# One transformer block in float32 on one core: three layer-norm transposes moved from TensorE to VectorE and HBM, and tiles 5 to 8 reordered

## The chip, the core and the metric

The kernel runs on one core of a Trainium2 chip. The core has five engines, each with its own instruction queue that is worked off in program order: TensorE (PE) multiplies matrices and writes to PSUM, VectorE (DVE) and ScalarE (ACT) do elementwise work, GpSimd (POOL) does some more of it, and SyncE (SP) issues the transfers between HBM and on-chip memory. Engines wait for one another through semaphores. The metric is the device time of one launch in microseconds (us); smaller is better. The kernel before takes 554.39 us, the median of 3 runs (554.28 to 555.3).

## The reference, cut to what matters

The input x has 2048 tokens of 512 channels. A modulation vector of six parts is made from c; then a linear attention with 32 heads of 16 channels is added to x, and then a bilinear feed-forward network of width 1376. Both have a modulated layer norm in front.

```python
mod = (_silu(c) @ w_mod).reshape(c.shape[0], 6, 1, -1)
sa, ca, ga, sb, cb, gb = (mod[:, 0], mod[:, 1], ..., mod[:, 5])
h = _layernorm(x) * (1 + ca) + sa                    # first layer norm
q, k, v = split(h @ wqkv)                            # 32 heads of 16
phi = lambda t: jnp.where(t > 0, t + 1, jnp.exp(t)) + 1e-6
kv = einsum("bhsd,bhse->bhde", phi(k), v);  z = sum over s of phi(k)
o = (phi(q) @ kv) / (phi(q) . z + 1e-6)
x = x + ga * (o @ wo)
h = _layernorm(x) * (1 + cb) + sb                    # second layer norm
x = x + gb * (((h @ w_gate) * (h @ w_up)) @ w_down)
```

## The kernel before, in words

The 2048 tokens lie in four chunks (0 to 3) of four tiles of 128 tokens, so there are tiles 0 to 15. Every float32 product is computed from a high part h, rounded to the format that TensorE reads fast, and a low part l, the rest: h by h, h by l and l by h, so three matmuls for each 128 channels of depth. A product of one tile with a 512 by 512 weight has twelve matmuls (`product`, L203).

A product needs the normalized activations with channels on the partitions, and they come with tokens on the partitions. So each chunk's norm is transposed. In `Norm.transpose` (L289) TensorE turns sixteen blocks of 128 by 128 for a chunk, four for each of the four channel groups k, into a PSUM bank each; `Norm.modulated` (L302) scales and shifts the bank on ScalarE into f, casts f to h (VectorE or ScalarE) and takes l = f - h on VectorE.

The kernel has another way to turn a tile, used already for the queries of tiles 4 to 15 and for the second norm of chunks 2 and 3: the columns are written in an order that groups blocks of 32 (`xhat_blocks`, L275), the tile is stored to HBM, loaded back with its blocks of 32 rows moved to other partitions (`move_out`, `move_in`, L719 and L725: one store, four loads), and VectorE transposes the blocks of 32 by 32 (`turn_v` L733, `flip` L899). `flipped` (L904) then scales and shifts one channel group out of the four turned tiles in the buffer `wide`; it reads all four of them.

*The first loop (L525)* runs over the tiles i. TensorE does the key projection of tile i+2 (`proj(i + 2, wk)`), in passes 3, 4, 6 and 7 a query projection as well (`q_at`, L521), and then `t_tile(i)`, the twelve matmuls that add tile i's phi(k) times normalized x to the attention state. ScalarE and VectorE split the normalized x (`k_split_x`), split phi(k) (`k_split`), make phi of the projections (`k_phi`, `q_a`, `q_b`), add up phi (`z_add`) and do the jobs of `extra` (L509): splits of the value and output weights, and parts of the modulation vector (`mod_part`). The norm of chunk ch+1 is prepared inside chunk ch's passes: statistics in passes j = 2 and 3 of the chunk before, scale and offset for all four tiles at once (`rstd_of`, with a power on GpSimd, and `nmr_of`) in j = 3, the normalized tiles (`xhat`) in j = 3 and 0, and the transposes in j = 0 and 1, eight at a time, between the halves of `t_tile`. The key projection of tile 8 is the first that needs chunk 2, that of tile 12 the first that needs chunk 3.

*After the loop* the order of the work is written out by hand (L1207 on). `gate_up(ch, f)` makes the products with the gate and up weights for one of three lone column groups f0, f1, f2 of width 128, 128 and 96, and the function that it returns multiplies and splits them; `down` multiplies with the down weights. `y_step(i)` adds the attention output of tile i to x (`y_a`, twelve matmuls), readies the next tile and takes the row sums of the tile before for the second norm (`y_b`). `den_a`, `den_b` and `den_c` make the attention's denominators of a chunk and divide by them; `ready` is `den_c` and the store of `move_out`. `ln2_nx` and `ln2_turn` normalize and turn a chunk's second norm. From L1348 on a Strassen-like scheme works on the rest of the feed-forward columns (L1030), with operands kept in HBM (`kept`).

All work tiles share one pool of 94 buffers (`NB`), in PSUM there are 4 + 4 banks, and all transfers go through the queue of SyncE in program order.

## Time and profile before

| what | value |
|---|---|
| median of 3 runs | 554.39 us (554.28 to 555.3) |
| the profiled execution | 554.37 us |
| its span, first to last instruction | 552.7 us |
| TensorE busy | 547.0 us (99%) |
| VectorE busy | 373.6 us (68%) |
| ScalarE busy | 291.7 us (53%) |
| GpSimd busy | 203.4 us (37%) |
| HBM read, written | 42.60 MB, 15.20 MB |
| granted TensorE clock | full in every slice |

Busy times are of one profiled execution. A timeline row has the start in us from the first instruction, the duration, the engine, the line of the kernel, the operation and its tiles, and in brackets the idle time before it and what ended it. Matmuls are pipelined: a matmul of 512 columns is shown as 0.39 us, while the next one starts 0.23 us after it; the distance of starts is what counts. In the same way an operation of VectorE or ScalarE overlaps the end of the one before by about 0.1 us. L12 is line 12 of the kernel.

### The profile page before, as it was taken

How to read it: one execution, taken by the hardware profiler on the slowest of the kernel's cores; microseconds unless marked ns; L12 is line 12 of the kernel's file. 1: busy time of each engine (PE TensorE's matmuls, PEld its weight loads, DVE VectorE, ACT ScalarE, POOL GpSimd, SP SyncE). 2: the span in 40 equal slices, each digit the busy share in tenths (PEclk: the TensorE clock that was granted, in tenths of full speed). 3: DMA queues.
4: the chain of work that ended last, by engine and by line, in shares of the span. 5: the costliest groups of instructions: out<-in, count | busy, mean ns of one | idle time of the engine just before them, and what ended most of it. 6: DMA issues, size and time to landing. Idle time of an engine off the chain costs nothing.

```text
span 552.7 us, 7324 instructions
## 1 busy us (share of the span) xinstructions
PE 547.0 (99%) x2488; PEld 449.2 (81%) x2488; DVE 373.6 (68%) x610; ACT 291.7 (53%) x539; POOL 203.4 (37%) x204
## 2 busy tenths in 40 slices
PE   8999999999999999999999999999999999999997
PEld 7788888888888878878888888877888888888886
DVE  7896968986887886778776576985444444434434
ACT  3695856646476667566684545454443444444110
POOL 2000000102003201057596666766666546446200
PEclk9999999999999999999999999999999999999999
DMA  8900203320503205845545071690434222200004
GB/s 284 387 15 2 76 20 103 108 77 1 157 2 133 96 5 186 267 145 135 160 111 155 0 230 38 216 322 2 133 116 132 59 57 59 58 20 0 1 0 152
DMA packets 58373, 58.28 MB, mean 105 GB/s; under 512 B 7328, under 2 KB 38304, under 8 KB 58336
## 3 DMA queue, kind: packets, MB, share of 16 engines
q1 hardware_dynamic: 58336, 57.83, 33.2%
q8 instruction: 19, 0.31, 0.2%
q14 instruction: 18, 0.15, 0.1%
HBM read 42.60 MB, written 15.20 MB: 105 GB/s over the span
## 4 chain that ended last, share of the span: by engine, by line
PE 99%; DVE 0%; issue 0%
PE bank L1030 33%; PE acc L766 7%; PE acc L1110 6%; PE acc L1111 6%; PE acc L1112 6%; PE bank L207 5%; PE bank L209 5%; PE bank L208 5%; PE acc L375 3%; PE acc L374 3%; PE acc L373 3%; PE bank L849 2%; PE bank L851 2%; PE bank L850 2%; PE acc L146 2%; PE bank L293 2%
## 5 line engine op out<-in xcount | busy, mean ns | idle before, releaser
L1030 PE MATMUL bank<-h,w 128*128 128x512 f32 (+1 forms) x798 | 184.7, 390 | 0.0
L1030 PEld LDWEIGHTS bank<-h,w 128*128 128x128 f32 (+1 forms) x798 | 148.4, 186 | 33.4 <-ACT bank L1035 0.7
L1035 ACT ACTIVATE bank<-bank 128x512 f32<-128x512 f32 (+1 forms) x38 | 22.2, 583 | 139.6 <-PE bank L1030 139.5
L836 DVE TENSOR_TENSOR x<-acc,x 128x512 f32<-128x512 f32 (+1 forms) x73 | 48.8, 682 | 48.4 <-PE acc L1112 47.7
L1016 POOL TENSOR_TENSOR w<-raw,w 128x256 fp32r<-128x256 f32 (+3 forms) x38 | 40.9, 1077 | 91.0 <-ACT w L1009 91.0
L1111 PE MATMUL acc<-w,kh 128*128 128x512 f32 (+2 forms) x154 | 59.6, 387 | 0.0
L1110 PE MATMUL acc<-w,kh 128*128 128x512 f32 (+2 forms) x154 | 59.6, 387 | 0.0
L1112 PE MATMUL acc<-w,kl 128*128 128x512 f32 (+2 forms) x154 | 59.5, 386 | 0.0
L263 POOL TENSOR_TENSOR rstd<-ve,half 128x4 f32<-128x4 f32 (+1 forms) x10 | 11.0, 1103 | 121.8 <-DVE ve L262 69.6
L195 POOL TENSOR_TENSOR w<-raw,w 128x512 fp32r<-128x512 f32 (+1 forms) x25 | 35.1, 1409 | 52.2 <-ACT w L194 47.3
L1016 POOL TENSOR_TENSOR w<-t,w 128x512 fp32r<-128x512 f32 (+1 forms) x38 | 49.2, 1318 | 0.0
L195 DVE TENSOR_TENSOR kl<-u,kh 128x512 fp32r<-128x512 f32 (+1 forms) x38 | 26.4, 736 | 30.6 <-ACT kh L194 30.6
L207 PE MATMUL bank<-w,h 128*128 128x512 f32 x104 | 40.9, 394 | 0.0
L209 PE MATMUL bank<-w,h 128*128 128x512 f32 x104 | 40.6, 391 | 0.0
L208 PE MATMUL bank<-w,h 128*128 128x512 f32 x104 | 40.6, 390 | 0.0
L766 PE MATMUL acc<-w,xh 128*128 128x512 f32 x120 | 37.4, 393 | 0.0
L1089 DVE TENSOR_TENSOR u<-bank,u 128x512 f32<-128x512 f32 (+1 forms) x19 | 13.1, 691 | 31.6 <-PE bank L1030 25.1
L1110 PEld LDWEIGHTS acc<-w,kh 128*128 128x128 f32 (+1 forms) x154 | 28.9, 188 | 6.0
L1112 PEld LDWEIGHTS acc<-w,kl 128*128 128x128 f32 (+1 forms) x154 | 28.9, 188 | 5.9
L1111 PEld LDWEIGHTS acc<-w,kh 128*128 128x128 f32 (+1 forms) x154 | 28.9, 188 | 5.9
L998 POOL TENSOR_TENSOR t<-raw,t 128x256 f32<-128x256 f32 (+1 forms) x34 | 25.9, 761 | 1.4
L766 PEld LDWEIGHTS acc<-w,xh 128*128 128x128 f32 x120 | 22.2, 188 | 4.6
(211 smaller groups left out, 1116.5 us busy)
## 6 DMA issues: line engine op xcount, KB each, us to landing
raw<-in_w_mod_dram SPq DMA_DIRECT2D x24, 256.0 KB, 3.7
raw<-in_B_w_down_dram SPq DMA_DIRECT2D x20, 256.0 KB, 3.2
raw<-in_B_w_gate_dram SPq DMA_DIRECT2D x36, 128.0 KB, 3.4
raw<-in_B_w_up_dram SPq DMA_DIRECT2D x36, 128.0 KB, 3.4
x<-in_A_x_dram SPq DMA_DIRECT2D x16, 256.0 KB, 5.4
out_dram<-x SPq DMA_DIRECT2D x15, 256.0 KB, 2.6
raw<-in_A_wqkv_dram SPq DMA_DIRECT2D x12, 256.0 KB, 5.4
moved<-h SPq DMA_DIRECT2D x12, 256.0 KB, 2.1
```

What stands on the lines that cost most here:

```text
L195: (low or nc.vector).tensor_tensor(l, src, f32(h), op=ALU.subtract)
L207: nc.tensor.matmul(ps, ah, bh, start=i == 0, stop=False)
L208: nc.tensor.matmul(ps, ah, bl, start=False, stop=False)
L209: nc.tensor.matmul(ps, al, bh, start=False, stop=i == n - 1)
L766: nc.tensor.matmul(yps[i], x, y, start=False, stop=k == KD - 1 and x is al, skip_group_check=True)
L836: nc.vector.tensor_tensor(xt[:, a:b], dn[j][:, a:b], xt[:, a:b], op=ALU.add)
L998: sub = lambda out, x, y: (on or nc.gpsimd).tensor_tensor(out, x, y, op=ALU.subtract)
L1016: sub = lambda out, x, y: (on or nc.gpsimd).tensor_tensor(out, x, f32(y), op=ALU.subtract)
L1030: mm = lambda x, y, **kw: nc.tensor.matmul(ps, x[:, k], y, skip_group_check=True, **kw)
L1110: nc.tensor.matmul(ps, hh[:, a:b], dh[:n, c:d], start=i == 0, stop=False)
L1111: nc.tensor.matmul(ps, hh[:, a:b], dl[:n, c:d], start=False, stop=False)
L1112: nc.tensor.matmul(ps, hl[:, a:b], dh[:n, c:d], start=False, stop=i == len(hs) - 1)
```

## The change

The first norms of chunks 2 and 3 (`LIFTED`) and the second norm of chunk 1 are no longer transposed by TensorE. Their tiles are written in the block order, stored (`lift_out`), loaded back regrouped (`lift_in`), turned by VectorE into `wide` (`lift_turn`), and each channel group is scaled and shifted by ScalarE (`lift_row`) and split (`lift_parts`). The existing functions `move_out`, `move_in`, `flip` and `flipped` are now written with these helpers (left out below).

In the first loop the scale and offset of a chunk's four tiles come in two halves: tiles 0 and 1 are normalized and stored at the start of pass j = 3, tiles 2 and 3 at its end; the loads follow there; VectorE turns tiles 0 and 1 at the end of pass j = 0 and tiles 2 and 3 in pass j = 1, and the row passes stand right behind. In pass 6 the query projection is put ahead of the key projection of tile 8. The splits of the output weights go from passes 12 and 13 to passes 14 and 15.

After the loop, the denominators of chunk 2 are made in halves, the first one earlier; tiles 4 to 7 of the attention output follow one another and the third gate/up product comes behind them; chunk 1's second norm is stored and loaded while that product and the down product run, and turned around tiles 8 and 9. The down product of chunk 0 goes over its four tiles for f0 and f1 first and then for f2. Some small operations change places.

```diff
@@ -317,6 +317,41 @@
                 self.t[k] = (h, l)
 
 
+    LIFTED = (2, 3)
+
+    def lift_out(name, x):
+        to = tc.dram_tile([P, D], F32, name=name)
+        nc.sync.dma_start(to, x)
+        return to
+
+    def lift_in(of):
+
+        v = of.rearrange("(m i) (q c) -> q i m c", i=BL, c=P)
+        u = B("u")
+        for q in range(NQ):
+            nc.sync.dma_start(u[q * BL:(q + 1) * BL].rearrange("i (m c) -> i m c", c=P), v[q])
+        return u
+
+    def lift_turn(j, u):
+        nc.vector.transpose(wide[:, j].rearrange("p (m s i) -> p m s i", m=NQ, i=BL),
+                            u.rearrange("p (m s i) -> p m s i", m=NQ, i=BL))
+
+    def lift_row(k, scale, shift):
+        f = B("f")
+        nc.scalar.activation(f.rearrange("p (x i) -> p x i", i=BL),
+                             wide.rearrange("p j (m s i) -> p (j m) s i", m=NQ, i=BL)[:, :, k],
+                             AF.Identity, scale=scale[:, k:k + 1], bias=shift[:, k:k + 1])
+        return f
+
+    def lift_parts(k, f, cast=True):
+        h, l = B("h", dt=F32R), B("h", dt=F32R)
+        if k % 2 and cast:
+            nc.vector.tensor_copy(h, f)
+        else:
+            nc.scalar.activation(h, f, AF.Copy)
+        nc.vector.tensor_tensor(l, f, f32(h), op=ALU.subtract)
+        return h, l
+
     NT = NCH * NJ
     norm = [Norm(xts[0])]
     wk, wq, wv = [], [], []
@@ -343,7 +378,13 @@
     def k_split_x(i):
         ch, j = divmod(i, NJ)
         kx[i] = [B("xh", dt=F32R), B("xl", dt=F32R)]
-        split(norm[ch].n[j], *kx[i])
+        if ch not in LIFTED:
+            split(norm[ch].n[j], *kx[i])
+            return
+        x = by_row(norm[ch].n[j])
+        h, l = (t.rearrange("p (s q i) -> p s q i", q=NQ, i=BL) for t in kx[i])
+        nc.scalar.activation(h, x, AF.Copy)
+        nc.vector.tensor_tensor(l, x, f32(h), op=ALU.subtract)
 
     def k_phi(i, ps):
         phi = B("phi")
@@ -514,20 +555,23 @@
              9: lambda: (mod_part(2, 2, 3), mod_load(4)),
              10: lambda: (pairs.update({2: split_raw(accs[2], low=nc.gpsimd)}), mod_part(3, 0, 1, 2), raw_o.extend(load(wo_v[k], "raw") for k in range(2))),
              11: lambda: (mod_part(3, 3), mod_part(4, 0, 1), rows.update({2: mod_row(2, pairs[2])}), raw_o.extend(load(wo_v[k], "raw") for k in range(2, KD))),
-             12: lambda: (mod_part(4, 2, 3), wo_s.extend(split_raw(x) for x in raw_o[:2]), cols.update({3: col_out(3, mod_col(accs[3], bank()), 0.0)}), mod_load(5)),
-             13: lambda: (mod_part(5, 0, 1, 2), wo_s.extend(split_raw(x) for x in raw_o[2:]), cols.update({4: col_out(4, mod_col(accs[4], bank()), 1.0)})),
-             14: lambda: (mod_part(5, 3),)}
+             12: lambda: (mod_part(4, 2, 3), cols.update({3: col_out(3, mod_col(accs[3], bank()), 0.0)}), mod_load(5)),
+             13: lambda: (mod_part(5, 0, 1, 2), cols.update({4: col_out(4, mod_col(accs[4], bank()), 1.0)})),
+             14: lambda: (mod_part(5, 3), wo_s.extend(split_raw(x) for x in raw_o[:2])),
+             15: lambda: wo_s.extend(split_raw(x) for x in raw_o[2:])}
     pairs = {}
     q_at = {3: 0, 4: 1, 6: 2, 7: 3}
     ahead = {2: k_ps[2], 3: k_ps[3]}
-    turn_at = {4 * ch + j: (ch + 1, 2 * j, 2 * j + 1) for ch in range(1, NCH - 1) for j in range(2)}
-    turn_at.update({1: (1, 0, 1), 2: (1, 2, 3)})
+    turn_at = {1: (1, 0, 1), 2: (1, 2, 3)}
     for i in range(NT):
         ch, j = divmod(i, NJ)
         done = 0
+        up = ch + 1 if 0 < ch < NCH - 1 else None
+        if i == 6:
+            qps = proj(q_at[i], wq)
         if i > 2:
             ahead[i + 2] = proj(i + 2, wk) if i + 2 < NT else proj(i + 6 - NT, wq)
-        if i in q_at:
+        if i in q_at and i != 6:
             qps = proj(q_at[i], wq)
         def turn_x():
             to, *ks = turn_at[i]
@@ -535,18 +579,23 @@
             nx.modulated(ca, sa, *ks, cast=nc.vector)
             norm[to:] = [nx]
 
-        fresh = i > 0 and ch + 1 < NCH and j == 0
         if i == 2:
             turn_x()
             wq.extend(split_blocks(r) for r in raw_q)
-        if fresh:
-            nx.xhat(2)
+        if ch + 2 < NCH and j == 3:
+            nx = nx2
+            nx.nmr_of(0, 2)
+            nx.xhat_blocks(0, 1)
+            lifts = [lift_out(f"first_{ch}_{n}", nx.n[n]) for n in range(2)]
         if 0 < i < NT - 1:
             k_split_x(i + 1)
-        if fresh:
-            nx.xhat(3)
-        if 0 < i < NT - 1:
             k_split(i + 1)
+        if up and j == 1:
+            lift_turn(2, lifts[2])
+            lift_turn(3, lifts[3])
+            for k in range(KD):
+                nx.t[k] = lift_parts(k, lift_row(k, ca, sa), cast=up == 2)
+            norm[up:] = [nx]
         if i in turn_at and i != 2:
             t_tile(i, 0, 1)
             done = 2
@@ -558,12 +607,10 @@
         if ch + 2 < NCH and j == 2:
             nx2 = Norm(xts[ch + 2])
             nx2.stats(0, 1)
+            nx2.rstd_of(0, 2)
         if ch + 2 < NCH and j == 3:
-            nx = nx2
             nx.stats(2, 3)
-            nx.rstd_of()
-            nx.nmr_of()
-            nx.xhat(0, 1)
+            nx.rstd_of(2, 4)
         if i + 2 < NT:
             k_phi(i + 2, ahead.pop(i + 2))
         else:
@@ -572,6 +619,12 @@
         if i in q_at:
             q_a(q_at[i], qps)
             q_b(q_at[i])
+        if ch + 2 < NCH and j == 3:
+            nx.nmr_of(2, 4)
+            nx.xhat_blocks(2, 3)
+            lifts[0], lifts[1] = lift_in(lifts[0]), lift_in(lifts[1])
+            lifts += [lift_out(f"first_{ch}_{n}", nx.n[n]) for n in (2, 3)]
+            lifts[2], lifts[3] = lift_in(lifts[2]), lift_in(lifts[3])
         if i + 1 < NT:
             z_add(i + 1)
         if i == NT - 2:
@@ -583,6 +636,9 @@
             zq = B("z")
             nc.gpsimd.tensor_copy(zq.rearrange("p (q s i) -> p q s i", q=NQ, i=BL), by_block(zb))
         t_tile(i, *range(done, KD))
+        if up and j == 0:
+            lift_turn(0, lifts[0])
+            lift_turn(1, lifts[1])
         if i in extra:
             extra[i]()
     ga, sb, cb = rows[2], cols[3], cols[4]
@@ -618,9 +674,10 @@
             den_p(ch, j, on=on)
             den_r(ch, j)
 
-    def den_b(ch):
-        nc.vector.tensor_tensor(dens[ch], dens[ch], (den0q if ch * NJ in FLIPPED else den0).unsqueeze(1).to_broadcast([P, NJ, NH]), op=ALU.add)
-        nc.vector.reciprocal(dens[ch], dens[ch])
+    def den_b(ch, a=0, b=NJ):
+        d = dens[ch][:, a:b]
+        nc.vector.tensor_tensor(d, d, (den0q if ch * NJ in FLIPPED else den0).unsqueeze(1).to_broadcast([P, b - a, NH]), op=ALU.add)
+        nc.vector.reciprocal(d, d)
 
     def den_c(*tiles):
 
...
@@ -1237,6 +1285,7 @@
     split_down(f0, nc.gpsimd)
     ready(7)
     move_in(5)
+    den_a(2, 0, 1, on=nc.vector)
     ln2_turn(0, 0, 1, cast=nc.vector)
     q_b(13)
     ps15 = proj(15, wq, acc_bank)
@@ -1258,32 +1307,59 @@
     split_gu(f2)
     g = gate_up(0, f1)
     turn_v(6)
-    den_a(2, 0, on=nc.vector)
+    turn_h(5)
+    turn_l(5)
+    y_seed(5)
     split_down(f1, nc.gpsimd)
     g()
-    y_step(4, lambda: scale_down(f2), lambda: den_a(2, 1, on=nc.vector))
+    y_step(4, lambda: turn_v(7))
+    den_b(2, 0, 2)
+    ready(8, 9)
+    move_in(8, 9)
+    y_step(5, lambda: scale_down(f2))
+    y_step(6, lambda: den_a(2, 2, 3, on=nc.vector))
+    y_step(7, turn=False, seed=False)
+    den_b(2, 2, 4)
     g = gate_up(0, f2)
-    split_down(f2)
-    turn_h(6)
-    turn_l(6)
-    y_seed(6)
-    turn_v(7)
+    norm2[1].rstd_of(0, 3)
+    y_b(7)
+    ready(10)
+    norm2[1].nmr_of(0, 3)
+    norm2[1].rstd_of(3, 4)
+    norm2[1].xhat_blocks(0, 1, 2)
+    lifts = [lift_out(f"second_1_{n}", norm2[1].n[n]) for n in range(3)]
+    ready(11)
+    norm2[1].nmr_of(3, 4)
+    norm2[1].xhat_blocks(3)
+    lifts.append(lift_out("second_1_3", norm2[1].n[3]))
+    for n in range(NJ):
+        lifts[n] = lift_in(lifts[n])
+    move_in(10, 11)
+    split_down(f2, nc.gpsimd)
     g()
-    den_a(2, 2, on=nc.vector)
-    y_step(5, lambda: den_a(2, 3, on=nc.vector))
-    y_step(6, lambda: den_b(2), lambda: ready(8))
-    y_step(7, lambda: ready(9), lambda: move_in(8), turn=False, seed=False)
-    y_b(7)
-    norm2[1].rstd_of()
-    ready(10)
-    ln2_nx(1)
-    take = down(0, ahead={1: (lambda: move_in(9), lambda: ready(11)),
-                          3: (lambda: turned_v(8), lambda: y_seed(8, bank), lambda: move_in(10, 11), lambda: turn_v(9))})
+    for i in (8, 9):
+        turn_v(i)
+        turn_h(i)
+        turn_l(i)
+    lift_turn(0, lifts[0])
+    lift_turn(1, lifts[1])
+    take = down(0, parts=((f0, f1), (f2,)), ahead={6: (lambda: y_seed(8, bank),)})
     take()
-    ln2_turn(1, 0, 1)
-    y_step(8, lambda: turn_v(10))
-    ln2_turn(1, 2, 3)
-    y_step(9, lambda: turn_v(11))
+    y_step(8, turn=False)
+    lift_turn(2, lifts[2])
+    lift_turn(3, lifts[3])
+    fs = [lift_row(0, cb, sb)]
+    norm2[1].t[0] = lift_parts(0, fs[0])
+    y_step(9, seed=None)
+    for k in range(1, KD):
+        fs.append(lift_row(k, cb, sb))
+        norm2[1].t[k] = lift_parts(k, fs[k])
+    for k in range(KD):
+        nc.sync.dma_start(kept[1][k], fs[k])
+    turn_v(10)
+    turn_h(10)
+    turn_l(10)
+    y_seed(10)
     side.update(plain_side((0, 1)))
     first = [Left((0, 1), k).into(side) for k in range(KH)]
     for x in first:
@@ -1293,6 +1369,7 @@
     g = gate_up(1, f0)
     den_a(3, 0, 1, on=nc.vector)
     g()
+    turn_v(11)
     y_step(10)
     g = gate_up(1, f1)
     den_a(3, 2, 3, on=nc.vector)
@@ -1317,8 +1394,8 @@
     first[0].sum("s1", "s3", on=nc.gpsimd)
     g(lambda: turn_v(13))
     y_seed(13, y_bank)
+    turn_h(13)
     norm2[2].xhat_blocks(2, 3)
-    turn_h(13)
     turn_l(13)
     move_in(14, 15)
     stow(2, 0, 1, 2, 3)
```

17 lines of the change are left out of this document (4 added, 13 removed).

## The prediction

> **What bounds the kernel now.** I read the page's busy times first, then its chain of work that ended last, then the waits of TensorE, then the rows of TensorE's own transposes.
>
> ```profile
> span 552.7 us, 7324 instructions
> PE 547.0 (99%) x2488; PEld 449.2 (81%) x2488; DVE 373.6 (68%) x610; ACT 291.7 (53%) x539; POOL 203.4 (37%) x204
> PE acc L146 <- DVE w L141: 2.0, 1, 2.0
> L293 PE MATMUL bank<-ident,n x80: 270/272/274, 32.0 to 219.5; 128*128 128x128 f32 x80
> 55.95 0.87 PE bank L293 x8
> ```
>
> The first rows are the page's busy times, the third the only wait of TensorE (PE) in the view of waits, the fourth the transposes, the last a piece of the chain. The reader is to see that TensorE is busy 99% of the span and waited once, 2.0 us at the very start. After that it always found its operands ready. So every matmul taken away is a gain in full, and every operand that comes late is a loss in full, because TensorE works in program order. The profiled run took 554.37 us, its span of 552.7 and 1.7 around it; the median of the three runs is 554.39, so the sum can be made on the profiled run.
>
> **What is removed.** The change takes out 48 of the 80 transposes of L293: 16 each for chunk 2's and chunk 3's first norm and for chunk 1's second. Eight of them hold TensorE for 0.87 us, so 48 are worth 6 x 0.87 = 5.22 us. All other matmuls stay in number; some change places. This is the whole gain that the change can have.
>
> **What takes their place.** For each chunk: four stores to HBM, sixteen loads back, four block transposes on VectorE (DVE), four strided row passes on ScalarE (ACT), then high and low parts. None of it is on TensorE, so in itself it costs nothing. The question is whether it ends before TensorE asks for it.
>
> *Chunk 2 (asked for by the key projection of tile 8).* Rows of the timelines of TensorE, VectorE and ScalarE, and of the two lines that already do the new operations elsewhere:
>
> ```profile
> 64.39 0.39 PE L207 MATMUL bank<-w,h 128*128 128x512 f32 x1
> 67.11 0.40 PE L207 MATMUL bank<-w,h 128*128 128x512 f32 x1
> 69.91 0.39 PE L373 MATMUL acc<-kh,xh 128*128 128x512 f32 x1
> 57.24 0.43 DVE L313 CAST h<-f 128x512 fp32r<-128x512 f32 x1
> 59.37 0.68 DVE L341 SCALAR_TENSOR_TENSOR phi<-bank,phi 128x512 f32<-128x512 f32 x1
> 62.62 0.68 DVE L365 SCALAR_TENSOR_TENSOR kl<-phi,kh 128x512 fp32r<-128x512 f32 x1
> 182.77 0.70 DVE L736 STREAM_TRANSPOSE f<-u 128x512 f32<-128x512 f32 x1
> 183.40 1.42 DVE L341 SCALAR_TENSOR_TENSOR h<-acc,h 128x512 f32<-128x512 f32 x2
> L907 ACT ACTIVATE f<-wide,col,col x8: 800/805/817, 302.8 to 345.7; 128x512 f32<-128x512 f32 x8
> 50.15 1.52 ACT L272 ACTIVATE n<-x,nmr,rstd 128x512 f32<-128x512 f32 x2 [4.27 <-DVE nmr L267]
> 181.81 1.14 ACT L194 ACTIVATE w<-raw 128x512 fp32r<-128x512 f32 x2
> 131.73 2.49 DVE L195 TENSOR_TENSOR w<-n,w 128x512 fp32r<-128x512 f32 x4
> ```
>
> Tile 8's key projection starts at 64.39 and takes twelve matmuls, 2.72 us to 67.11, 0.227 each. In the new order 16 transposes ahead of it are gone (-1.74) and the query projection of tile 2, 67.11 to 69.91 = 2.80 us, goes first: TensorE asks for chunk 2 at 65.45. VectorE ends tile 6's split at 62.62 + 0.68. Four operations ahead of it go (57.24 to 59.37, 2.13 us) and two block transposes come (0.63 each from one start to the next, 182.77 to 183.40): it starts that split at 61.75 and is through at 62.4. Two more block transposes end at 63.7. Only then can ScalarE start, because each row pass reads all four turned tiles. From one start to the next ScalarE needs 0.72 for a row pass (two take 1.52, one 0.80) and 0.53 for a cast (two take 1.14, one 0.61); VectorE needs 0.60 for a subtraction (four take 2.49). The first row and cast end at 65.05, in time; four rows and two casts end near 67.7; VectorE's last cast and subtraction end at 68.9. TensorE wants that last part for the last of the twelve matmuls, at 67.95. **Wait: 0.95 us.** Bounds: 0 and 2.
>
> *Chunk 3 (asked for by the key projection of tile 12).* More rows of the same timelines, one of the DMA queue, and the landing times of stores and loads of this kind:
>
> ```profile
> 93.65 0.39 PE L207 MATMUL bank<-w,h 128*128 128x512 f32 x1
> 68.73 0.69 DVE L242 BATCH_NORM_STATS2 st<-x 128x6 f32<-128x512 f32 x1
> 70.34 0.67 DVE L341 SCALAR_TENSOR_TENSOR phi<-bank,phi 128x512 f32<-128x512 f32 x1
> 76.15 0.17 DVE L262 TENSOR_SCALAR ve<-mv 128x4 f32<-128x4 f32 x1
> 77.53 0.16 DVE L267 SCALAR_TENSOR_TENSOR nmr<-mv,rstd 128x4 f32<-128x4 f32 x1 [1.21 <-POOL rstd L263]
> 90.33 0.75 DVE L164 SCALAR_TENSOR_TENSOR f<-raw,sc,f 128x512 f32<-128x512 f32 x1
> moved<-h SPq DMA_DIRECT2D x12, 256.0 KB, 2.1
> u<-moved SPq DMA_DIRECT2D x48, 64.0 KB, 2.0
> 176.09 1.83 SPq L731 DMA_DIRECT2D u<-moved  x4
> ```
>
> Here no query projection is put in front. Tile 12's projection stands at 93.65 now; 32 transposes less (-3.49) and the wait just found (+0.95) make 91.1. VectorE, from 68.8: nine operations at 0.60, two statistics (1.61 for both, 68.73 to 70.34) and a small one, 76.2. There the first two tiles' scale is formed, ScalarE regroups them (1.45) and splits tile 8's x (0.6), 78.4; VectorE takes two subtractions and the other two statistics, 81.3; the power on GpSimd takes 76.15 to 77.53 = 1.4; so the last two tiles' scale comes at 82.9. Before, all four came at 77.53: halving puts the second half 5.4 us later, because VectorE reaches its statistics only after waits on ScalarE. From there two ways run side by side:
> - ScalarE regroups the two tiles until 84.5; the last store lands 2.1 later, 86.6; eight loads issue one after another at 0.455 each from 86.0, the last at 89.1, and land 2.0 later, near 91.2.
> - VectorE, held until ScalarE has regrouped and split a weight (85.1), takes three subtractions, waits for tile 10's phi (87.35), then phi, sum, two block transposes, two modulation parts (0.5 and 0.7), two splits: 92.2, and the last two block transposes, 93.5.
>
> The first row pass and cast (all four casts are ScalarE's here) end at 95.0, 3.9 us after TensorE asks. Four rounds at 1.24 and the last subtraction end at 99.4; the projection ends at 99.7 instead of 91.1 + 2.72 = 93.85. **Wait: 5.8 us**, 3.9 in one piece. Bounds: by the loads alone the first row could start at 91.9, a wait of 4.2; with VectorE 1.5 us later than counted, 7.3. A lower bound of 2 would need the second half's scale near 79.
>
> *The output weights' split,* two iterations later: two casts and two subtractions in the last loop pass, 1.2 us of VectorE ahead of the state's splits. The row at 131.73 above is these four splits, and this one is the first matmul that uses them:
>
> ```profile
> 134.59 0.22 PE L207 MATMUL bank<-w,w 128*128 128x128 f32 x1
> ```
>
> The four low parts end at 134.2; TensorE wants the first at 134.8 and the last at 135.8. Pushed by 1.2 they end at 135.4: 0 us, up to 0.5 if the cover fails.
>
> *Chunk 1's second norm, and tiles 5 to 8.* TensorE's order becomes two gate/up products, tiles 4, 5, 6, 7, the third product, the down product, tiles 8 and 9, the next gate/up.
>
> ```profile
> 190.47 0.62 PE L766 MATMUL acc<-w,xh 128*128 128x512 f32 x2
> 193.19 0.39 PE L849 MATMUL bank<-h,w 128*96 128x512 f32 x1
> 192.22 0.68 DVE L858 TENSOR_TENSOR phi<-bank,phi 128x512 f32<-128x512 f32 x1
> 193.60 0.69 DVE L195 TENSOR_TENSOR kl<-phi,kh 128x512 fp32r<-128x512 f32 x1 [0.70 <-ACT kh L194]
> 204.56 0.95 DVE L623 RECIPROCAL den<-den 128x128 f32<-128x128 f32 x1
> 222.50 0.39 PE L849 MATMUL bank<-h,w 128*128 128x512 f32 x1
> 215.23 2.45 DVE L836 TENSOR_TENSOR x<-acc,x 128x512 f32<-128x512 f32 x4
> 247.17 1.25 DVE L195 TENSOR_TENSOR kl<-phi,kh 96x512 fp32r<-96x512 f32 x1
> 230.51 0.58 ACT L250 ACTIVATE x<-acc 128x512 f32<-128x512 f32 x1
> 231.80 0.19 ACT L251 ACTIVATION_READ_ACCUMULATOR acc<-acc,sums 128x1 f32 x1
> 249.82 0.40 PE L875 MATMUL acc<-w,kh 96*128 96x512 f32 x1
> ```
>
> A tile takes 2.72 (190.47 to 193.19), so tile 6 stands at 195.9 and needs its low part at 196.4. Without the denominator work that stands before it now, the second product's multiply starts at 191.4 instead of 192.22 and its low part ends 2.05 later; then come a block transpose, half a denominator (half of 0.95 and a small sum), two scalings at 0.60 and the subtraction: 196.7. **Wait 0.35** (0 to 1). The next gate/up starts at 222.50 - 1.74 + 0.35 = 221.1. VectorE ends the four evictions at 217.9 or so and two block transposes at 219.2; ScalarE makes row and cast 0 by 220.4, then tile 8's two statistics passes (1.48, 230.51 to 231.99), then row 1: its cast is there at 223.1 and its low part at 223.8, wanted at 222.45 and 222.7. **Wait 1.2** (0 to 2.5). Behind it VectorE carries four more transposes (2.5 us) toward the third product of this chunk, whose low part ends at 248.4 and is wanted at 249.8: 1.4 spare. I take **0.5** (0 to 1.6). The denominators of tiles 8 and 9, moved up, fill 3.5 us in which VectorE waits now for the second norm of chunk 0; cost 0, or 1 if late. The low part of the third product's down weights goes to GpSimd, which has nothing else there but two powers, and tile 13's cast trades places with two row passes: 0 each.
>
> **The sum.** -5.22 + 0.95 + 5.8 + 0.35 + 1.2 + 0.5 = +3.6: 554.37 + 3.6 = 558.0 us. Its own range, from the bounds, is 555.5 to 561.
>
> **The rivals.** First, *chunk 3 arrives in time* (other side). Place: tile 12's key projection; price 5.8; it decides where the second half's scale comes by 79 instead of 82.9. Then the sum is 552.2, and with the small waits gone too 549.2. For it speaks that VectorE is busy 68% only; against it that its idle time lies in waits on ScalarE which the halving makes longer. Chance 0.20. Halfway, with a wait of 3 there, lies no change: 0.07.
>
> Second, *the clock falls in the wait*. This row of the chain is the start of TensorE's work:
>
> ```profile
> 2.00 8.63 PE acc L146 x26
> ```
>
> 26 matmuls took 8.63 us, where 26 x 0.227 = 5.9 is the later pace: an array that has stood still lost 2.7 us. The 3.9 us in one piece before tile 12 could cost that again: 560.7. The Trainium skill, "TensorE: Matmul & The Clock Gate" (Why this matters for your kernels), asks for no idle gap over about 3 us between bursts, since one idle window brings back the half clock. The trace agrees at the start only, and its granted clock reads full there too. Chance 0.12.
>
> Third, *the loads wait for buffers*. Modulation weights queue for tile buffers now:
>
> ```profile
> 80.91 14.45 SPq L113 DMA_DIRECT2D raw<-in_w_mod_dram  x8
> ```
>
> Eight issues spread over 14.45 us where eight loads of L731 take 3.7. If chunk 3's sixteen loads meet the same, the turn starts some 3 us later: 561. Chance 0.11.
>
> **How the numbers follow.** The forecast holds 0.50, the rivals 0.20 + 0.07, 0.12 and 0.11. This kernel's runs tell about 0.2% (1.1 us) from no change; slower holds 0.50 + 0.12 + 0.11 less 0.03 for the forecast's lower edge, 0.70; same 0.09; faster 0.21. The range cuts the better half of the first rival and the worse part of the last two: 551 to 562.
>
> **What would show it.** L293 falls from 80 to 32 rows. TensorE shows idle time before L207, about 1 us near 66 and 4 to 6 us near 91 to 99, released by VectorE's low part or ScalarE's cast, and 1 to 2 us before L849 near 222. If TensorE stays without waits, the VectorE and ScalarE sequence is wrong and the time is near 549. If the matmuls after the wait stand 0.45 us apart, the second rival holds; if block transposes wait for DMA well after 91.2, the third.

## The result, and the profile after

The changed kernel takes 560.72 us (median; 560.28 to 563.38) against 554.47 for the kernel before on the same chip: a ratio of 1.0116 with a 95% interval of 1.0094 to 1.0138. That is 6.25 us slower. The forecast was 558.0 with a range of 551 to 562, and "slower" at 0.70. The profiled execution took 560.78 us, so the traces can be compared directly: 560.78 - 554.37 = +6.4. Two single executions of later kernels, 919.59 and 683.04 us at a granted clock of 0.56 and 0.75, are left out of the medians below.

From the page of the kernel after, the busy times and the granted clock by slices:

```profile
span 559.0 us, 7384 instructions
PE 547.8 (98%) x2440; PEld 445.1 (80%) x2440; DVE 382.8 (68%) x625; ACT 294.1 (53%) x543; POOL 206.5 (37%) x208
PEclk9999998999999999999999999999999999999999
```

TensorE has 48 instructions fewer (2440 instead of 2488), as the change says, and yet its busy time is 0.8 us longer. The seventh digit of the clock is an 8: in that slice, 84 to 98 us, the granted clock was below 90%. The views of TensorE's waits, first for 60 to 105 us, then for 195 to 275 us (columns: who waited, for whom, us in total, times, longest):

```profile
PE bank L207 <- ACT h L351: 3.5, 1, 3.5
```

```profile
PE bank L1078 <- ACT bank L1083: 0.7, 1, 0.7
PE acc L930 <- DVE kl L195: 0.7, 1, 0.7
PE acc L928 <- ACT kh L194: 0.3, 1, 0.3
PE bank L903 <- DVE h L352: 0.2, 1, 0.2
```

Before, TensorE waited once, at the very start. Now there are five more waits. The longest stands where the forecast put it, in front of the key projection of tile 12. Rows of TensorE's timeline there:

```profile
90.88 0.39 PE L416 MATMUL acc<-kl,xh 128*128 128x512 f32 x1
94.77 0.80 PE L207 MATMUL bank<-w,h 128*128 128x512 f32 x1 [3.51 <-ACT h L351]
95.36 0.63 PE L208 MATMUL bank<-w,h 128*128 128x512 f32 x1
95.79 0.63 PE L209 MATMUL bank<-w,h 128*128 128x512 f32 x1
96.22 0.71 PE L207 MATMUL bank<-w,h 128*128 128x512 f32 x1
...
98.95 0.71 PE L207 MATMUL bank<-w,h 128*128 128x512 f32 x1
...
99.89 0.59 PE L209 MATMUL bank<-w,h 128*128 128x512 f32 x1
100.32 0.40 PE L414 MATMUL acc<-kh,xh 128*128 128x512 f32 x1
```

The projection could have started at 91.1 and taken 2.72; it ends at 100.32. The loss is 9.21 - 2.72 = 6.5 us. A little over half is the hole from 91.1 to 94.77; the rest is that the four groups of three matmuls start 1.36 to 1.45 us apart where they need 0.68. What sets that pace is in ScalarE's and VectorE's timelines of the same stretch:

```profile
91.85 1.30 DVE L336 STREAM_TRANSPOSE wide<-u 128x512 f32<-128x512 f32 x2
93.25 0.81 ACT L341 ACTIVATE f<-wide,col,col 128x512 f32<-128x512 f32 x1 [4.66 <-DVE wide L336]
94.09 0.63 ACT L351 ACTIVATE h<-f 128x512 fp32r<-128x512 f32 x1
94.63 0.80 ACT L341 ACTIVATE f<-wide,col,col 128x512 f32<-128x512 f32 x1
95.46 0.63 ACT L351 ACTIVATE h<-f 128x512 fp32r<-128x512 f32 x1
```

The last two block transposes start at 91.85, the first row pass 1.4 later, and from row pass to row pass it takes ScalarE 1.37 us, because each cast starts only when the whole row pass in front of it is through (0.84 after its start).

At chunk 2 the same kind of loss is small. Two rows of TensorE, the first matmul of tile 8's key projection and the first one behind it, and the row of VectorE's last low part:

```profile
65.70 0.39 PE L207 MATMUL bank<-w,h 128*128 128x512 f32 x1
69.20 0.39 PE L414 MATMUL acc<-kh,xh 128*128 128x512 f32 x1
68.12 0.69 DVE L352 TENSOR_TENSOR h<-f,h 128x512 fp32r<-128x512 f32 x1
```

The projection takes 3.50 where it needs 2.72, a loss of 0.78.

Summed over the kernel, by the starts of equal matmuls in the two traces:

| place | forecast, us | measured, us |
|---|---|---|
| 48 transposes gone | -5.22 | -5.22 (L293: 32 instead of 80) |
| the kernel's start, in front of anything that was changed | none | 0.3 |
| chunk 2, tile 8's key projection | 0.95 | 0.78 |
| chunk 3, tile 12's key projection | 5.8 | 6.5 |
| output weights' split, end of the loop | 0 (to 0.5) | 0.37 |
| tile 6's low part | 0.35 | 0.33 |
| gate and up product of chunk 1 | 1.2 | 0.93 |
| third product's low part | 0.5 (to 1.6) | 1.64 |
| the first block of the later products (L1078) | none | 1.0 |
| sum | +3.6 | +6.6 |

The last matmul of the kernel comes 6.34 us later than before, so the table accounts for the whole to 0.3. The 0.3 at the start is a difference between two executions and not an effect of the change: TensorE is that much later from about 8 us on (55.86 against 55.56 just before the first transposes that are gone).

### The profile page after: what moved, and what is told of

Read it like the earlier page. It is cut to its first block, busy times and chain, and to the rows that moved or that the text cites. A ratio compares the mean times of both kernels' runs of the same rounds, so it can differ in the third digit from the quotient of the medians.

```text
span 559.0 us, 7384 instructions
## 1 busy us (share of the span) xinstructions
PE 547.8 (98%) x2440; PEld 445.1 (80%) x2440; DVE 382.8 (68%) x625; ACT 294.1 (53%) x543; POOL 206.5 (37%) x208
## 4 chain that ended last, share of the span: by engine, by line
PE 82%; ACT 6%; DVE 6%; DMA 2%; SPq 2%; issue 2%; DVEq 0%; ACTq 0%
PE bank L1078 32%; PE acc L1158 6%; PE acc L1159 6%; PE acc L1160 6%; PE bank L207 5%; PE bank L209 4%; PE bank L208 4%; PE acc L819 3%; PE acc L416 2%; PE acc L415 2%; PE acc L414 2%; PE acc L146 2%; SPq L332 2%; DVE h L195 1%; ACT n L279 1%
## 5 line engine op out<-in xcount | busy, mean ns | idle before, releaser
L1078 PE MATMUL bank<-h,w 128*128 128x512 f32 (+1 forms) x798 | 185.0, 390 | 0.7 <-ACT bank L1083 0.7
L1078 PEld LDWEIGHTS bank<-h,w 128*128 128x128 f32 (+1 forms) x798 | 148.3, 186 | 34.4 <-ACT bank L1083 1.8
L1083 ACT ACTIVATE bank<-bank 128x512 f32<-128x512 f32 (+1 forms) x38 | 22.1, 583 | 139.1 <-PE bank L1078 139.0
L263 POOL TENSOR_TENSOR rstd<-ve,half 128x2 f32<-128x2 f32 (+3 forms) x13 | 12.6, 970 | 123.0 <-DVE ve L262 73.3
L195 POOL TENSOR_TENSOR w<-raw,w 128x512 fp32r<-128x512 f32 (+1 forms) x26 | 36.4, 1404 | 56.0 <-ACT w L194 51.5
L207 PE MATMUL bank<-w,h 128*128 128x512 f32 x104 | 42.4, 408 | 3.5 <-ACT h L351 3.5
L209 PE MATMUL bank<-w,h 128*128 128x512 f32 x104 | 41.8, 402 | 0.0
L208 PE MATMUL bank<-w,h 128*128 128x512 f32 x104 | 41.6, 400 | 0.0
L207 PEld LDWEIGHTS bank<-w,h 128*128 128x128 f32 x104 | 19.9, 192 | 9.1 <-ACT h L351 5.0
```

The source lines that it names most:

```text
L195: (low or nc.vector).tensor_tensor(l, src, f32(h), op=ALU.subtract)
L207: nc.tensor.matmul(ps, ah, bh, start=i == 0, stop=False)
L208: nc.tensor.matmul(ps, ah, bl, start=False, stop=False)
L209: nc.tensor.matmul(ps, al, bh, start=False, stop=i == n - 1)
L1078: mm = lambda x, y, **kw: nc.tensor.matmul(ps, x[:, k], y, skip_group_check=True, **kw)
```

## The experiments

Times are medians; each ratio is to the kernel before, run on the same chip at the same time. "Over before" is the difference of these two medians; it is what is compared from kernel to kernel.

**Chunk 3 on TensorE again.** Theory: lateness at tile 12 is most of the loss. Rival: the loss moves to the next thing that is late.

```diff
-    LIFTED = (2, 3)
+    LIFTED = (2,)
-    turn_at = {1: (1, 0, 1), 2: (1, 2, 3)}
+    turn_at = {1: (1, 0, 1), 2: (1, 2, 3), 8: (3, 0, 1), 9: (3, 2, 3)}
...
+            if fresh:
+                nx.xhat(2)
```

> The change with one part undone: chunk 3's first norm is turned by TensorE again, as before; chunk 2's first and chunk 1's second norm stay with VectorE. Theory of lateness (chunk 3's parts come after TensorE asks for them): the 6.5 us lost before and in tile 12's key projection go, 16 transposes (1.74) come back: 560.7 - 4.7 = 556.0 us. Rival, a general burden (VectorE's added work slows the whole loop and what follows): less than 2 us go, 559 or more.

Measured: 559.70, ratio 1.0084 (1.0066 to 1.0101), 4.8 over before. A miss; the rival's time, 559 or more, came out. The two longest of TensorE's waits behind its start:

```profile
PE acc L832 <- ACT acc L823: 1.8, 1, 1.8
PE bank L293 <- ACT n L272: 1.6, 2, 0.9
```

The wait at tile 12 is gone, but the transposes themselves now wait (L293), because VectorE is still behind from chunk 2 and forms chunk 3's scale 2.3 us later than in the kernel before (79.88 instead of 77.53). A new wait of 1.8 appears at a product near 250 us, for a seed from ScalarE; there VectorE's block transpose in front (247.97) had waited 1.77 for its load. So what was taken away at tile 12 did not come off the total: other operands were late behind it, at single places and not all along the kernel.

**The loop of after with the products of before.** The part of the file behind `f0, f1, f2 = lone` is before's.

> The change in the first loop alone; all that stands after the loop is as before (chunk 1's second norm by TensorE, old order of tiles and denominators). Theory that each place makes its own waits: the waits of 0.33, 0.93, 1.64 and 1.0 us after 190 us go (3.9) and 1.74 of transposes come back: 558.5 us. Rival, that the later waits are inherited from the loop's delay: they stay and the time is 561 to 562.4.

Measured: 558.30, ratio 1.0063 (1.0044 to 1.0081), 3.35 over before, as expected. TensorE's waits are the 3.5 at tile 12 and one of 0.6 at tile 13 of the products. This kernel is the base of all runs from the fifth on but one; their expectations call it the 558.6 us kernel, after a median that still holds the execution of 683.04.

**The hole filled.** Is the half clock after the hole worth anything by itself?

```diff
+        if i == 12 and w is wk:
+            for _ in range(16):
+                nc.tensor.matmul(ps, wk[0][0][:, :P], wk[0][0], start=True, stop=True)
```

> The change with 16 matmuls whose result is thrown away (3.6 us of TensorE work) in front of tile 12's key projection, so that TensorE does not stand still there; all operands come as before. Theory of lateness: the clock stays full, but the parts come only at 1.37 us a channel group from ScalarE, so the projection ends at 99.8 instead of 100.3: 560.3 us, 0.5 less. Rival, the clock: the half clock costs what it cost at the start of the kernel, 2.7 us: 558.0 us.

Measured: 562.15, ratio 1.0126 (1.0105 to 1.0147). No gain; its interval overlaps that of after. The profiled execution took 560.62 at a granted clock of 1.0 (after's took 560.78); the other three took 562.08 to 562.85 at 0.994 to 0.997, so in them the clock fell at a place that no trace here shows, and the median is not that of a kernel with a full clock. Two views of the kernels after and filled: granted clock in stretches (columns: stretch, us, busy us of TensorE, weight loads, VectorE, ScalarE and GpSimd, granted clock, DMA share, GB/s), first after:

```profile
92.00:96.00 4.00, 1.23 (x3) 0.79 (x3) 1.84 (x3) 2.69 (x5) 0.00 (x0) 0.69 1.01 361
96.00:98.00 2.00, 2.00 (x5) 1.28 (x5) 1.20 (x2) 1.97 (x4) 0.00 (x0) 0.50 0.73 229
98.00:100.40 2.40, 2.40 (x7) 1.49 (x7) 1.27 (x3) 2.33 (x5) 0.00 (x0) 0.52 0.00 0
```

then the filled kernel, and its matmuls:

```profile
96.00:98.00 2.00, 1.85 (x6) 0.67 (x4) 0.96 (x2) 1.94 (x4) 0.00 (x0) 1.00 0.51 165
```

```profile
90.56 3.79 PE L366 MATMUL bank<-w 128*128 128x512 f32 x16
94.22 0.50 PE L207 MATMUL bank<-w,h 128*128 128x512 f32 x1
95.59 0.50 PE L207 MATMUL bank<-w,h 128*128 128x512 f32 x1
...
98.33 0.50 PE L207 MATMUL bank<-w,h 128*128 128x512 f32 x1
...
99.39 0.39 PE L417 MATMUL acc<-kh,xh 128*128 128x512 f32 x1
```

The clock did fall to half in after, as the Trainium skill, "TensorE: Matmul & The Clock Gate" (Why this matters for your kernels), says of an idle gap over about 3 us; the trace agrees, 0.50 granted in and behind a gap of 3.5 us. That does not make a shorter gap safe: in the next run the clock fell after two gaps of about 0.9 us, and the measurement decides. With the hole filled it stays at 1.00, and still the groups start 1.37 apart: they wait for ScalarE's next cast. From the point where the projection could start to its end it is 99.39 - 90.56 = 8.83 us at full clock and 9.21 at half. So the half clock cost 0.4 us, most of it in the last group, where no further cast is waited for, and not the 2.7 of the rival. Even this 0.4 is gone again at the gate and up product of chunk 1 (225 to 227 us), where TensorE then waits longer.

**Two query projections in front of tile 12.** Tile 4's and 5's query projections are moved there from the loop's end.

> The change with the query projections of tiles 4 and 5 moved from the last two passes of the first loop in front of tile 12's key projection: TensorE has 5.45 us of other work while chunk 3 is on its way. Theory of lateness: of the 6.5 us about 0.7 stay, and up to 0.5 come at the end of the loop where these two projections covered the split of the state: 555 us. Rival, that the loads wait for buffers which TensorE's progress frees: a wait of 3 us or more stays at tile 12, 558 or more.

Measured: 558.36, ratio 1.006 (1.0043 to 1.0077), 3.4 over before. The loss at tile 12 shrank to 0.7, as expected (36 matmuls from 90.86 to 99.73, where 8.16 are needed), so the rival's wait of 3 did not come. Expected was 555, though; TensorE's rows at the loop's end say where the rest went:

```profile
124.94 0.50 PE L183 MATMUL bank<-w,ones_r 128*128 128x512 f32 x1 [0.89 <-ACT w L194]
126.29 0.71 PE L183 MATMUL bank<-w,ones_r 128*128 128x512 f32 x1 [0.85 <-POOL w L195]
126.80 0.63 PE L414 MATMUL acc<-kh,xh 128*128 128x512 f32 x1
127.23 0.63 PE L415 MATMUL acc<-kh,xl 128*128 128x512 f32 x1
```

L183 is the row sum at the loop's end. The two projections had covered the chain from the last feature map through its sum and split to that product; with them gone it is bare, and the wait comes back there. Behind it the clock falls once more; the view of the granted clock has 0.57 on average for 126 to 130 us, which is 3.4 us at half:

```profile
126.00:130.00 4.00, 3.71 (x9) 2.93 (x10) 3.11 (x5) 2.70 (x5) 0.85 (x2) 0.57 0.00 0
```

From 126.80 to 129.79 the state products stand 0.43 apart instead of 0.23, another 1.4 us. Here no operand is waited for, so the half clock costs its full price.

**State products first.** Here the cover is taken from work that is ready at the same place.

```diff
+        if i in (6, 10):
+            t_tile(i, *range(KD))
+            done = KD
         if i > 2:
             ahead[i + 2] = proj(i + 2, wk) if i + 2 < NT else proj(i + 6 - NT, wq)
```

> After's loop with before's products behind it (the 558.6 us kernel), and in tiles 6 and 10 the twelve state products (t_tile), whose operands are long ready, are put ahead of the next chunk's first key projection (tiles 8 and 12). Theory 'lateness': the operands of chunk 3 come when VectorE and ScalarE have them, whatever TensorE does meanwhile, so 2.72 us of ready work in front of the wait take 2.7 off it, and the 1.0 us wait at tile 8 is gone; less up to 0.4 because tile 10's low key part is ready only at 91.4. 555.5 (555.0 to 556.5). Rival 'the wait is only moved' (what stood behind tile 12's projection as cover is missing later): 558.3 or more.

Measured: 556.39, ratio 1.0034 (1.0022 to 1.0047), 2.0 over before: in the range expected, at its upper end. TensorE's waits in the loop are now 0.9 at tile 10's low input part and 0.2 at tile 12. Of the base's 3.35 us over before this one change of order gets 1.4 back.

**The second half's scale earlier.** The forecast's first rival said that chunk 3 is in time if that scale comes by 79. Here it does.

```diff
+            nx.stats(2, 3)
+            nx.rstd_of(2, 4)
         if 0 < i < NT - 1:
             k_split_x(i + 1)
             k_split(i + 1)
+        if ch + 2 < NCH and j == 3:
+            nx.nmr_of(2, 4)
+            nx.xhat_blocks(2, 3)
...
```

> The 558.6 us kernel with the statistics of tiles 2 and 3 of the next chunk in front of the splits of the current tile, so that the second half's scale comes at about 79 instead of 82; stores, loads and turns keep their order, and so does VectorE's list behind it. Theory 'VectorE's list': in the 558.6 us kernel the turns of tiles 2 and 3 began at 91.30, the moment the low key part in front of them ended, with the loads landed by about 90.2 to 90.9; an earlier scale brings the loads forward by at most 0.7 and the turns by nothing: 558.6 (558.2 to 559.0). Rival, the condition given in the prediction ('in time if the second half's scale comes by 79'): the wait at tile 12 falls by 2 to 3, 556 (555.5 to 556.6).

Measured: 557.56, ratio 1.0056 (1.0041 to 1.0071), 3.2 over before. That is 0.2 less than its base, which these runs can't tell from nothing. VectorE's rows, first of the base, then of this kernel:

```profile
81.98 0.15 DVE L267 SCALAR_TENSOR_TENSOR nmr<-mv,rstd 128x2 f32<-128x2 f32 x1
91.30 1.30 DVE L336 STREAM_TRANSPOSE wide<-u 128x512 f32<-128x512 f32 x2
```

```profile
78.44 0.15 DVE L267 SCALAR_TENSOR_TENSOR nmr<-mv,rstd 128x2 f32<-128x2 f32 x1
90.27 1.30 DVE L336 STREAM_TRANSPOSE wide<-u 128x512 f32<-128x512 f32 x2
```

The scale comes 3.5 us earlier, at 78.4, and the turns only 1.0. They start in both kernels the moment the operation in front of them ends. The rival's condition was wrong: VectorE's list holds the turns, not the scale. The 1.0 comes from the list too. Half of it is chunk 2's: the edit moves that chunk's statistics as well, TensorE loses 0.5 less at tile 8, and all that follows is 0.5 earlier. The other half is that the two statistics now fill a time in which VectorE waited for ScalarE. (Expected was that the turns move by nothing.)

**Turns first, and a second queue.**

```diff
-            lifts[2], lifts[3] = lift_in(lifts[2]), lift_in(lifts[3])
+            lifts[2], lifts[3] = lift_in(lifts[2]), lift_in(lifts[3], nc.gpsimd)
...
             lift_turn(1, lifts[1])
+            if up == 3:
+                lift_turn(2, lifts[2])
+                lift_turn(3, lifts[3])
```

> The last kernel (early scale) with two more edits: the loads of the fourth tile go through GpSimd's queue, which is idle there, and the turns of tiles 2 and 3 of chunk 3 stand right behind those of 0 and 1, in front of the modulation sums (1.2 us) and of tile 10's low parts (1.2 us). Theory 'VectorE's list': turns 2 and 3 at about 89.0 instead of 91.3, first row at 90.4 instead of 92.7, and the last group, which sets the end of tile 12's projection, 2.3 earlier: 556.3 (555.8 to 557.0). Theory 'loads': the loads land no earlier than 90, and the gain is 1 or less: 557.6 to 558.6.

Measured: 560.77, ratio 1.0113 (1.0098 to 1.0128): worse than either theory gave. The rows of this kernel for VectorE, GpSimd's and SyncE's queues:

```profile
93.86 0.71 DVE L336 STREAM_TRANSPOSE wide<-u 128x512 f32<-128x512 f32 x1 [4.01 <-DMA u<-first]
87.02 2.20 POOL L332 DMA_DIRECT2D u<-first  x4 [8.24 <-ACT xh L386]
85.74 1.75 SPq L332 DMA_DIRECT2D u<-first  x4
87.60 10.32 SPq L113 DMA_DIRECT2D raw<-in_w_mod_dram  x8
```

Three turns went through early; the fourth waited 4.0 us for the four loads on GpSimd's queue. They began 1.3 later than SyncE's last four, took 0.55 each to issue, and moved beside the modulation weights that SyncE had started right behind its own loads. And VectorE, in order, held everything else behind that turn, so that TensorE's wait at tile 12 grew to 4.9. Whether the queue itself or the transfers beside it made the landing late was not separated. The Trainium skill, "Trainium Kernel Development and Optimization" (Key Constraints), says that DMAs of several queues run on the same 16 DMA engines and that a second queue saves only issue time; the trace fits that, and here even issue time was not saved: four issues took 2.20 on GpSimd's queue and 1.75 on SyncE's.

**All of it together.** State products first, early scale, the fourth tile on GpSimd's queue, turns 0 and 1 in front of the key feature map, casts shared by two engines, output weights split at tiles 12 and 13.

> All of it together on before's products behind the loop: state products first in tiles 6 and 10; early scale; fourth tile's loads on GpSimd's queue; in tile 8 turns 0 and 1 in front of the key feature map and turns 2 and 3 right behind it, the modulation sums behind chunk 3's rows; chunk 3's casts shared between ScalarE and VectorE as for chunk 2 (1.1 instead of 1.37 a group); output weights split at tiles 12 and 13 as before. If lateness is all that the loop lost, the 32 transposes come off: 554.95 - 3.48 + 0.6 (the wait at tile 13 found in the 558.6 us kernel) = 552.1 (551.5 to 553.5). If a wait of over 1 us stays at tile 12, or a new one comes at the loop's end: 553.5 to 555.

Measured: 557.62, ratio 1.0064 (1.0042 to 1.0086). A miss, above both expected ranges, for the same reason: the turn of the fourth tile waited 3.9 for GpSimd's loads, and tile 10's low part, behind it on VectorE, kept TensorE waiting 3.7. From issue to landing these loads took 4.2 us in the median, SyncE's 2.0.

**One queue.** The same with all loads on SyncE's queue, stores 2 and 3 between the loads of tiles 0 and 1, and turn 3 behind tile 10's low parts.

> The 'all in time' kernel without GpSimd's queue, whose four loads were issued from 85.6 and landed only at 92.5, beside the modulation weights that SyncE's queue had begun at 86.3: all loads on SyncE's queue again, in the order stores 0 and 1, loads of tile 0, stores 2 and 3, loads of tiles 1, 2, 3, so that the last load is issued by about 86.8, ahead of the modulation weights, and lands at about 88.7; turn 2 behind the key feature map of tile 10, turn 3 behind tile 10's low parts, rows from 90.5. Theory 'lateness': tile 12's projection starts without a wait at about 92.4 and the loop keeps its 3.48: 552.4 (551.6 to 553.6). Rival: a wait of 1 or more stays before tile 12's or tile 10's products, 553.8 to 555.5.

Measured: 554.87, ratio 1.0001 (0.9986 to 1.0015). Nothing is left of the wait before tile 12, and the loop's loss is nearly gone, but 552.4 it is not: the time is in the rival's range, though its wait stands one product further on. TensorE's one wait in the loop:

```profile
PE acc L415 <- DVE xl L387: 1.0, 1, 1.0
```

Tile 11's low input part now stands behind the modulation sums that had been moved out of chunk 3's way. With what the groups of tile 12 still lost (1.1) and this place (1.65, the wait and what the matmuls behind it lost) that is 2.75 of the 3.48 gained. Another 0.8 goes near 250 us, where tile 13 of the products waits for its low part as in the base (0.6).

**The products alone.** Before's loop with everything the change does behind it.

> Before's loop with everything that the change does behind it (denominators in halves, tiles 5 to 8 in a row, the second norm of chunk 1 turned by VectorE). Theory 'own waits': the 16 transposes (-1.74) and the waits found there in the trace of after (tile 6 0.33, gate and up product of chunk 1 0.93, third block's products 1.64, the first block after 1.0) stand on their own: -1.74 + 3.90 = +2.2, so 556.7 (556.1 to 557.3). Rival 'handed down': those waits come from the loop's lateness on VectorE and ScalarE; without it only the transposes count: 553 (552.6 to 554).

Measured: 556.82, ratio 1.0039 (1.0026 to 1.0052), 2.2 over before, as expected to a tenth. TensorE's waits in this kernel from 50 us on:

```profile
PE bank L1057 <- ACT bank L1062: 0.7, 1, 0.7
PE acc L909 <- DVE kl L195: 0.7, 1, 0.7
PE acc L907 <- ACT kh L194: 0.3, 1, 0.3
PE bank L882 <- DVE h L352: 0.2, 1, 0.2
```

They are the four of after, one for one, under other line numbers. They are not handed down from the loop; the second part of the change loses by itself: 1.74 gained, 3.9 lost. Loop (3.35) and products (2.2) add up to 5.5 of the 6.25.

**The list tidied.** On "one queue", the modulation sums of tiles 8 and 9 behind tile 11's parts, tile 9's feature sum behind chunk 3's rows.

> The 'one queue' kernel, in which tile 12's projection began at 93.4 without a wait but lost 1.1 in gaps between its groups, and 1.65 went at tile 11's low input part, which stood behind the modulation sums of tiles 8 and 9 on VectorE. Here those sums (2.6 us) stand behind tile 11's parts, and tile 9's sum of features behind chunk 3's rows. Theory 'lateness': tile 11's wait goes (-1.65) and the gaps at tile 12 shrink by up to 0.6: 553.0 (552.5 to 553.8). Rival 'the wait moves on to the next tile's parts': 554.2 to 555.

Measured: 555.21, ratio 1.0009 (1.0 to 1.0019). No wait is left at tiles 10 to 12; the next one is:

```profile
102.79 0.50 PE L183 MATMUL bank<-w,ones_r 128*128 128x512 f32 x1 [0.46 <-ACT w L194]
104.45 0.50 PE L183 MATMUL bank<-w,ones_r 128*128 128x512 f32 x1 [1.16 <-POOL w L195]
```

This is the row product of a modulation vector, whose sums are now late. The rival named beforehand, that the wait moves on, holds, 0.2 above its range; it went one step further than tile 12's parts.

**The lists apart.** Every modulation sum of tiles 10 to 14 one step later, and the products that need them one tile later.

```diff
+        if i == 11:
+            mod_part(3, 0, 1, 2)
+        if i == 12:
+            mod_part(3, 3)
+            mod_part(4, 0, 1)
...
-             11: lambda: (mod_part(3, 3), mod_part(4, 0, 1), rows.update({2: mod_row(2, pairs[2])}), raw_o...
+             12: lambda: (rows.update({2: mod_row(2, pairs[2])}), ...
```

> The 'list tidied' kernel had no wait left at tiles 10, 11 and 12 but a new one of 1.75 (102.8 to 104.8) at the row product of the third modulation vector, which now waited for the low part (GpSimd) of sums that VectorE had finished late. Here every modulation sum of tiles 10 to 14 stands one step later, behind the next tile's parts, and the vector's row and columns are taken one tile later, so that no product on TensorE stands behind them. Theory 'VectorE's list': the wait was one of order, and goes: 553.2 (552.6 to 554.0). Rival 'VectorE has no room': from 96 to 113 VectorE was busy without a gap in the last trace, so that putting one thing later makes the next one late, and the time stays at 554.3 to 555.5.

Measured: 554.53, ratio 0.9997 (0.9987 to 1.0006): the same as before, with 32 transposes fewer. At the last projection in front of the loop's end TensorE is 1.8 us ahead of the kernel before (121.4 against 123.2), and at the state products behind it it is level (126.4 in both): in between stands the row product of the feature sum, for whose two parts it waits 0.2 and 0.9 by the view of waits. The other half of the 3.48 was gone before that, most of it (1.3) in gaps between the groups of tile 12, whose projection takes 4.06 (92.89 to 96.95) instead of 2.72. The stretch from 96 to 125 us, first of this kernel, then of before:

```profile
96.00:125.00 29.00, 28.61 (x130) 22.77 (x130) 28.34 (x46) 16.50 (x29) 1.91 (x2) 1.00 0.24 78
```

```profile
96.00:125.00 29.00, 29.00 (x137) 24.21 (x136) 25.25 (x41) 15.34 (x26) 2.46 (x2) 1.00 0.30 96
```

The third pair is VectorE: 28.34 of 29 us, where it was 25.25. The second rival's time came out, and its condition fits: from 97 to 124.7 us VectorE has no idle time in this trace. Each order of its list tried here only chose which product waits. That no order would do is not shown: the last feature sum, which the row product needs by way of ScalarE (123.99) and GpSimd (124.70 to 125.97), starts at 123.27 behind modulation sums (120.70 to 122.76) of a vector that is first used behind the loop. Neither that exchange nor taking work off VectorE altogether (a feature sum on GpSimd, say) was tried, so whether the 3.48 can be freed stays open. None of the twelve kernels is faster than the one before.

## Why the prediction was right, step by step

Sign, place and kind were right: operands that come late at the places named, tile 12's key projection first. The time was 2.7 short, and these steps carry that.

- *What is removed: 5.22.* Right; 32 transposes are left.
- *Chunk 2, 0.95.* Measured 0.78. VectorE's last low part ends at 68.81, where 68.9 was forecast: the count of its list row by row held to a tenth. TensorE asked at 65.70 instead of 65.45, because it was 0.3 behind from the kernel's start.
- *Chunk 3, 5.8.* Measured 6.5. The asked-for time was right (91.1), with some luck, as the 0.3 at the start nearly made up for the smaller loss at chunk 2; the last low part (99.4 forecast) ends at 99.54. Two sizes were off and partly cancelled: the last block transposes ended at 93.15 and not 93.5, and a round of row pass and cast takes 1.37, not 1.24, because the cast waits for the whole row pass, while the pairs of rows it was priced from did not depend on each other. The other half of the miss is the half clock in the last group, 0.4.
- *The output weights' split, 0.* Measured 0.37, inside the bound of 0.5. The four low parts start at 137.41 instead of 131.73, so 5.7 later, while TensorE is 4.0 later there: they were pushed by 1.7 and not by 1.2, and the cover did not reach.
- *Tile 6, 0.35, and gate and up of chunk 1, 1.2.* Measured 0.33 and 0.93; both well inside their bounds.
- *The third product's low part, 0.5.* This is the term that failed most: 1.64, just past its bound of 1.6. By the prediction's own figures a push of 2.5 less a spare of 1.4 makes 1.1; the 0.5 has no working. And the push was larger. The multiply of the product in front, first in before, then in after:

```profile
236.37 0.69 DVE L858 TENSOR_TENSOR phi<-bank,phi 128x512 f32<-128x512 f32 x1 [0.20 <-PE bank L851]
243.47 0.68 DVE L911 TENSOR_TENSOR phi<-bank,phi 128x512 f32<-128x512 f32 x1
```

  It comes 7.1 later, where TensorE is 3.7 later, so VectorE's chain was pushed by 3.4 and not by the 2.5 counted; before, VectorE waited for TensorE here, now it does not. The waits in the chain behind it, 1.57 for ScalarE and 0.39 for a load, stand in the old trace too (1.58 and 0.20) and explain little.
- *Missing: 1.0 at the first block of the later products.* No step named it. There the eviction that frees a bank (L1083) stands on ScalarE behind an operation that waited 4.45 us for VectorE's statistics of the last tile; these stood behind four subtractions. They start 0.8 later against TensorE than before, and take 6.32 us instead of 5.49. The trace shows that chain; it was not tested alone. The sum stopped at the last operation the diff touches, while the lag went on.
- *The first rival, chunk 3 in time (0.20).* Its condition fell: with the scale at 78.4 the turns came 1.0 earlier only, half of it for another reason. With the wait really gone (the runs "one queue" to "lists apart") the loop's gain was used up at the next late product, so 552.2 is not what that rival would have given either.
- *The second, the clock (0.12).* Its time, 560.7, is the measured one, and its sign was seen: the matmuls behind the wait stand 0.43 apart. The time is a coincidence. The fall is real, but with the hole filled its price is 0.4 and not 2.7: an array that waits for operands at 1.37 us a group loses little by running at half. The sign was no test: the distance of matmuls inside a group does not tell what sets the distance of the groups. At the loop's end in "two query projections", where nothing else held the matmuls back, 3.4 us of half clock did cost 1.4.
- *The third, loads wait for buffers (0.11).* The turns started when VectorE's list let them, not when loads landed; it was not so here. In the two runs with GpSimd's queue a similar wait was made.
- *The range.* Its own range, 555.5 to 561, is not the plain sum of the bounds, which would go from about 553 to 564; the measured time lies just inside its upper end.

## What to carry to other kernels

Where TensorE is busy 99% of the time, taking matmuls away pays only as far as the other engines' ordered lists have room at that very place, not on average: VectorE was 68% busy over the kernel and, in the last run, 98% in the stretch behind tile 12. Follow each late operand past the last line of the diff, through every engine it hands its lag to, and price a chain of dependent instructions from a row in which they depend on each other. A time that comes out right does not choose between theories: here a rival's sum hit the measured time, and a run with its cause taken away brought nothing. Before buying off a wait, ask what the cover was doing: work moved from elsewhere uncovered a new wait, work that was ready at the same place did not.

## What the runs showed of the hardware

- In the kernel after, TensorE's last matmul before the hole starts at 90.88 and the next one at 94.77, with 3.5 us of idle time. The granted clock read 0.50 from 94 us on and was still at 0.52 on average from 98 to 100.4, while TensorE ran in groups with no idle time shown between them. Matmuls then stood 0.43 apart instead of 0.23.
- Shorter gaps did it too: in "two query projections" 3.4 us of half clock followed idle gaps of 0.89 and 0.85 us with one matmul between. One gap of 1.8 us (the first run, 1.00 granted from 245 to 258 us) and two of 0.22 and 0.85 ("lists apart", 1.00 from 123 to 131 us) did not; what decides is not shown.
- GpSimd's queue, with nothing else on it, took 0.55 us to issue a 64 KB load and 4.2 us (median of four) to land it; SyncE's took 0.43 and 2.0 (median of twelve) in the same trace ("all of it together"). The four moved beside the modulation weights, and no run had them alone.
- A subtraction of 128x512 on VectorE takes 0.69 us alone and up to 1.78 beside GpSimd's own work. In before, the same four take 1.49, 1.78, 1.78 and 0.68; the last one started at 260.3, when GpSimd was done (259.8). From VectorE's timeline of after, four that take 6.32 (1.22 and three of 1.78) while GpSimd is busy:

```profile
261.60 6.32 DVE L195 TENSOR_TENSOR h<-s,h 128x512 fp32r<-128x512 f32 x4
```
